# K chunks loaded in pairs wherever two neighbouring places come free within eight items

## The chip, the core and the metric

The kernel runs on one core of a Trainium2 chip. The core has engines with instruction streams of their own: PE (matmul, with its weight loads), DVE (vector), ACT (scalar), POOL, and SP (sync), which here only issues transfers. Sixteen DMA engines move the data between HBM and the on-chip memory. The metric is the device time of one execution in microseconds (us), lower is better.

## What is computed

Two layers, each an attention block over a cache followed by a small MLP block, for 8 sequences (batches) with one new token each, in bfloat16. Both layers read the same cache and the same weights.

```
q = (layernorm(x) @ wq)                    # 16 query heads of 256, 8 K/V heads, 2 query heads to each
scores = q . k_cache * 256**-0.5           # 4096 cached positions
o = softmax(scores) . v_cache
x = x + o @ wo                             # attention
h = gelu(layernorm(y) @ w1) ...            # MLP block B on y = layernorm(x); x = x + B(y)
x = attention; x = MLP; x = attention; x = MLP
```

With one position per sequence, the shifts in the MLP block bring in only zeros, so w1 and w2 add nothing and the kernel does not load them. The K and V caches are 8 x 8 x 4096 x 256 each, 128 MiB each.

## The kernel before

**Units, chunks and places.** The work is cut into units (layer `ps`, batch `b`, head pair `gp`): two K/V heads of one batch in one layer. A unit has four K chunks and four V chunks of 1 MiB (128 partitions by 8 KB). The on-chip memory holds `NC` = 17 places of one chunk each, side by side in one tile `places_t` (line 80), so two neighbouring places are one stretch of 16 KB per partition. A K chunk `c` holds, for each partition, the c-th 8 KB of a 32 KB run of the cache; so two neighbouring K chunks are 16 KB in a row in HBM too, and one transfer of 2 MiB can bring both, if two neighbouring places are free. Whole V chunks are 1 MiB transfers.

**What is kept.** Head pairs 2 and 3 (`keep`) of a batch are loaded in layer 0 and stay on the chip until layer 1 has used them: 14 of the 17 places hold them at the tightest point, a further V chunk is moved to PSUM (`inner`), and one is split between PSUM and the tile `rest` (`part`, `halfway`). Head pairs 0 and 1 (`free`) are loaded once for each layer.

**The list of items.** `block` and `first_kept` (lines 731 to 795) write out one list `items` of chunks in the order in which they are used. For each batch: units of `free` head pairs and the two kept units of layer 0; then a run of V chunks loaded as two halves of 512 KB (`narrow`, `halved`), under which the attention result of this batch goes through its output projection, the MLP and the next query (`chain`); then the kept K and V chunks again for layer 1, mixed with K chunks of the units that follow. I call the time from the kept chunks of layer 1 until the engines have caught up with the loads the catch-up.

**What an item does.** For a loaded K chunk, DVE transposes it in place (`transpose_k`, three instructions on line 1009). PE multiplies it with the query (`scores`, line 1024). For units named by `paired`, the scores wait for the second chunk of a pair and, where the two lie in neighbouring places, 32 matmuls of 256 columns do both; otherwise 64 of 128 columns. `late` says whose scores wait. Kept K chunks need no load and no transpose in layer 1; their first item's matmuls read both chunks of a pair. ACT takes the exponentials (line 1033). For a V chunk, PE multiplies the probabilities with it (line 1092).

**The list of loads.** `loads` is `items` without what is still on the chip. The main loop (line 1272) writes the instructions of one item, gives back the place or places that it used (lines 1463 to 1476), and calls `emit_loads` (line 930), which takes loads from the head of the list as long as it finds places. All of this is decided while the program is built: SP gets a fixed sequence of transfers, issued in order, each behind a wait for the last reader of its place. A transfer that waits holds up all behind it.

**How places are chosen.** For each place, `free_at` has the number of the item after which it comes free. `both_for` (line 900) looks whether a K chunk and its neighbour can be loaded as one: the mate must be among the next three loads, both places free or coming free within `AHEAD` = 4 items, and, where no pair is held yet, at least `QUEUED` = 7 loaded chunks still ahead of their use. The pair's places are then held, and `emit_loads` stops until both are free. Otherwise `place_for` (line 873) takes the first open place for the single chunk and may hold a neighbour for its mate, so that the scores can be done together although the chunks are loaded one by one. `paired` (line 850) excludes the units `begin[0]` and the last two of `final_units`.

At the start, `emit_loads(2)` issues the first two blocks of wq and `emit_loads(5)` (line 1133) five more transfers; then come the weights (lines 1134 to 1159), which are first used before item 12 (`kept_q`).

Of the kernel before, what the change touches and what calls it, by code (L numbers as in the profile page):

```python
# [17 lines left out]
def kernel(  # L18
# [27 lines left out]
    nc = tc.nc  # L46
# [3 lines left out]
    Dh = A_k_cache.shape[3]  # L50
# [10 lines left out]
    NC = 17  # L61
# [6 lines left out]
    PR = 6  # L68
# [10 lines left out]
    PB = 16 * Dh  # L79
    places_t = consts.tile([128, NC * PB], BF16, name="places")  # L80
    slots = [places_t[:, n * PB : (n + 1) * PB] for n in range(NC)]
    rest_t = consts.tile([128, (16 - PR) * Dh], BF16, name="rest")
# [603 lines left out]
    keep = sorted({gp for gp, _, _ in kept})  # L686
    free = [gp for gp in range(GP) if gp not in keep]
    assert Bn > 2 and free == [0, 1] and GP == 4
    begin = [(0, 0, 0), (0, 0, 1), (0, 1, 0), (0, 2, 0)]
# [10 lines left out]
    final_units = [(1, 5, 1), (1, 6, 1), (1, 7, 0), (1, 7, 1)]  # L700
# [18 lines left out]
    tasks, items, due = [], [], []  # L719
    number, narrow, halved, loose = {}, set(), set(), set()  # L720
# [101 lines left out]
    saved = {u for units in ahead for u in units}  # L822

    def stays(it):
        n, kv, c = it
        return (tasks[n][2], kv, c) in kept
# [5 lines left out]
    def halfway(it):  # L832
        n, kv, c = it
        return (tasks[n][2], kv, c) == part

    def here(it):

        return tasks[it[0]][0] == 1 and (stays(it) or inside(it) or halfway(it))

    loads = [it for it in items if not here(it)]  # L840


    places = list(range(NC))
    where = {}

    held = {}
    AHEAD = 4
    QUEUED = 7

    def paired(n, c):  # L850

        ps, _, gp = tasks[n]
        return gp in keep or tasks[n] in saved or tasks[n] in final_units[:2] + begin[1:]

    def late(it):

        n, kv, c = it
        return kv == 0 and paired(n, c) and not (tasks[n][0] == 1 and stays(it))
# [3 lines left out]
    used_at = {it: k for k, it in enumerate(items)}  # L862
# [7 lines left out]
    free_at = [-1] * NC  # L870
    now = [0]

    def place_for(it):

        n, kv, c = it
        if it in held:
            p = held.pop(it)
            if p not in places:
                held[it] = p
                return None  # L880
            places.remove(p)
        else:
            open_ = [p for p in places if p not in held.values()]
            if not open_:
                return None
            p = open_[0]
            if kv == 0 and c % 2 == 0 and paired(n, c):
                two = [
                    (max(free_at[q], now[0]), k, p1, q)
                    for k, p1 in enumerate(open_)  # L890
                    for q in (p1 + 1, p1 - 1)
                    if 0 <= q < NC and q not in held.values() and free_at[q] <= now[0] + AHEAD
                ]
                if two:
                    _, _, p, q = min(two)
                    held[n, 0, c + 1] = q
            places.remove(p)
        return p

    def both_for(it):  # L900

        n, kv, c = it
        mate = (n, 0, c + 1)
        if it not in held:
            if kv or c % 2 or not paired(n, c) or mate not in loads[:3]:
                return None
            open_ = [p for p in range(NC) if p in places or free_at[p] >= 0]
            two = [
                (max(free_at[q] if q not in places else -1 for q in (p, p + 1)), p)
                for p in open_  # L910
                if p + 1 in open_ and not {p, p + 1} & set(held.values())
            ]
            two = [t for t in two if t[0] <= now[0] + AHEAD]
            if not two or sum(used_at[i] > now[0] for i in where if i in used_at) < QUEUED:
                return None
            p = min(two)[1]
            held[it], held[mate] = p, p + 1
        if held.get(mate) != held[it] + 1:
            return None
        return held[it], mate  # L920

    def taken(it, p):

        where[it] = p
        n, kv, c = it
        if stays(it):
            where[tasks[n][1:], it[1:]] = p
        free_at[p] = again[tasks[n][1:], kv, c] if tasks[n][0] == 0 and stays(it) else used_at[it]

    def emit_loads(most=None):  # L930
        n = 0
        while loads and places and n != most:
            it = loads[0]
            both = both_for(it)
            if both:
                p, mate = both
                if p not in places or p + 1 not in places:
                    break
                for i, q in ((it, p), (mate, p + 1)):
                    loads.remove(i)  # L940
                    places.remove(q)
                    del held[i]
                    taken(i, q)
                _, b, gp = tasks[it[0]]
                nc.sync.dma_start(
                    places_t[:, p * PB : (p + 2) * PB],
                    A_k_cache[b, 2 * gp : 2 * gp + 2]
                    .rearrange("g s d -> (g s) d")
                    .rearrange("(p u z) d -> u p (z d)", u=2, z=32)[it[2] // 2],
                )  # L950
                n += 1
                continue
            p = place_for(it)
            if p is None:
                break
            del loads[0]
            taken(it, p)
            t, kv, c = it
            _, b, gp = tasks[t]
            dst = slots[p]  # L960
            n += 1
            if kv == 2:
                load_weights(dst, gp, b)
                continue
            rows = (A_v_cache if kv else A_k_cache)[b, 2 * gp : 2 * gp + 2].rearrange(
                "g s d -> (g s) d"
            )
            if kv:
                src = rows.rearrange("(a p y) d -> a p (y d)", a=4, y=16)[c]
            else:  # L970
                src = rows.rearrange("(p x y) d -> x p (y d)", x=4, y=16)[c]
            if halfway(it):
                nc.sync.dma_start(dst[:, 0 : PR * Dh], src[:, 0 : PR * Dh])
                nc.sync.dma_start(rest_t[:], src[:, PR * Dh :])
            elif loads and it not in halved:
                nc.sync.dma_start(dst, src)
            else:
                for y in range(2):
                    nc.sync.dma_start(
                        dst[:, 8 * Dh * y : 8 * Dh * (y + 1)], src[:, 8 * Dh * y : 8 * Dh * (y + 1)]  # L980
                    )

    def load_tail(dst, src):

# [4 lines left out]
    def load_weights(dst, kind, rows):  # L989

        if kind == "o":
            nc.sync.dma_start(
                dst[:, 0 : WI * D].rearrange("p (h x) -> p h x", x=2 * D),
                A_wo[0 : WI * 128].rearrange("(h p j) d -> p h (j d)", p=128, j=2),
            )
            return
        src = A_wq[:, HU * rows[0] : HU * rows[0] + HU]
        nc.sync.dma_start(
            dst[:, 0 : 3 * HU].rearrange("p (f c) -> p f c", f=3),
            src[0:384].rearrange("(f p) c -> p f c", f=3),  # L1000
        )
        load_tail(dst[:, 3 * HU : 3 * HU + HU // 2], src)
# [38 lines left out]
    def inner_words(slot):  # L1041

        return [(store[n][:], slot[:, 1024 * n : 1024 * n + 1024]) for n in range(4)]
# [228 lines left out]
    for idx, it in enumerate(items):  # L1272
# [9 lines left out]
        n, kv, c = it  # L1282
        ps, b, gp = tasks[n]
# [9 lines left out]
        kept_now = here(it)  # L1293
        p = where[(b, gp), (kv, c)] if kept_now else where[it]
# [3 lines left out]
        if kv == 2:  # L1298
            rows = b
# [25 lines left out]
        elif kv == 0:  # L1325
# [23 lines left out]
            x = c - c % 2  # L1349
# [4 lines left out]
            elif scored:  # L1354
                two = [
                    where[(b, gp), (0, k)] if kept_now else where[n, 0, k] for k in (x, x + 1)
                ]
# [14 lines left out]
        else:  # L1372
# [15 lines left out]
            if final and gp in free:  # L1388
                pv_cols(oc, slot, c, gp, psv[slot_of[n]])
                if c % 2 == 1:  # L1390

                    u = c // 2
# [70 lines left out]
        if kv == 2:  # L1463
            if gp == "q" or rows is not None:
                places.append(p)
        elif not (ps == 0 and stays(it)):
            if (ps, gp, kv, c) == (1, keep[1], 1, homes[0]):
                where[(b, part[0]), part[1:]] = p
                moves.extend(part_words(slot))
            elif (ps, gp, kv, c) == (1, keep[1], 1, homes[1]):  # L1470
                where[(b, inner[0]), inner[1:]] = p
                moves.extend(inner_words(slot))
            elif not late(it):
                places.append(p)
            elif c % 2:
                places.extend([where[n, 0, c - 1], p])
# [24 lines left out]
    for q in range(4):  # L1501
        for fc in range(4):
            at = min(128 * fc, D - 128)
# [134 lines left out]
```

## Time and profile before

| what | value |
|---|---|
| runs | 1037.08, 1040.58, 1041.28 us; median 1040.58 |
| profiled execution | 1038.57 us, its span 1036.0 us |
| moved by SP's queue | 419.66 MB in 73296 packets |
| HBM read over the span | 405 GB/s |
| mean granted clock of PE | 0.614 |
| K transfers of 2048 KB / 1024 KB | 49 / 94 |
| V transfers of 1024 / 512 KB | 87 / 194 |

The profile is one execution; its span runs from the first to the last instruction of the program. Engine shares are busy times over the span. "DMA" in the row of slices is the mean busy share of the sixteen DMA engines, "GB/s" what they moved in each of 40 slices of 25.9 us. In a row of instructions, "x" is the count, then busy us and the mean ns of one; behind the bar stands the idle time before them and what ended it. SP's waits for places are not a loss by themselves: as long as earlier transfers are queued, the DMA engines have work.

### The profile page before, as it was taken

The numbers are of one execution on the slowest core, as the hardware profiler recorded it, in microseconds if no ns is written. First come the engines' busy times: TensorE is split into PE (matmuls) and PEld (weight loads), VectorE is DVE, ScalarE is ACT, GpSimd is POOL, SyncE is SP. The second block draws the span as 40 slices with busy tenths as digits, with TensorE's granted clock in tenths as the row PEclk, the third lists the DMA queues.
The fourth block names the chain that finished last, engine by engine and source line by source line (L and its number), as shares of the span: only waits on it lengthen the run. The fifth ranks groups of instructions, "written<-read, shape, count | busy, mean of one in ns | idle before, by whom it ended". The sixth has DMA issues, their size and how long they took to land. (4 is left out here: it accounts for less than half of the span.)

```text
span 1036.0 us, 29893 instructions
## 1 busy us (share of the span) xinstructions
PE 668.8 (65%) x13219; PEld 429.1 (41%) x13219; DVE 597.9 (58%) x1407; ACT 211.5 (20%) x685; POOL 16.3 (2%) x27
## 2 busy tenths in 40 slices
PE   3154545875677557766775677567756774677775
PEld 2022322553345334533453345335533552345555
DVE  7054577258725971597259725782597259725582
ACT  1011111141214120412041214121412141214110
POOL 0000000000000000000000000000000000000000
PEclk9975555565667566655665565566555665556555
DMA  9999999999999999999999999999999999999994
GB/s 361 396 425 422 423 422 419 393 421 419 419 401 421 422 417 382 419 422 419 401 415 425 417 402 411 421 417 388 418 420 418 401 419 423 417 402 408 413 419 198
DMA packets 73472, 421.56 MB, mean 407 GB/s; under 512 B 7544, under 2 KB 13440, under 8 KB 43904
## 3 DMA queue, kind: packets, MB, share of 16 engines
q1 hardware_dynamic: 73296, 419.66, 99.1%
q8 instruction: 103, 1.69, 0.7%
q14 instruction: 25, 0.20, 0.0%
q10 hardware_dynamic: 48, 0.01, 0.0%
HBM read 419.63 MB, written 0.01 MB: 405 GB/s over the span
## 5 line engine op out<-in xcount | busy, mean ns | idle before, releaser
L1009 DVE STREAM_TRANSPOSE places<-places 128x512 uint32<-128x512 uint32 (+1 forms) x576 | 455.5, 854 | 58.8 <-DMA places<-in_A_k_cache_dram 58.6
L1024 PE MATMUL sc<-places,qbd 128*8 128x256 bf16 (+1 forms) x5248 | 248.8, 342 | 175.4 <-DVE places L1009 168.5
L1092 PE MATMUL o<-places,ptw 128*8 128x256 bf16 x3808 | 243.7, 380 | 111.5 <-DMA places<-in_A_v_cache_dram 82.2
L1024 PEld LDWEIGHTS <-qbd 128*8 128x8 bf16 x5248 | 134.0, 105 | 247.0 <-DVE places L1009 130.6
L1092 PEld LDWEIGHTS <-ptw 128*8 128x8 bf16 x3968 | 103.9, 102 | 175.1 <-issue 99.0
L1033 ACT ACTIVATE p_n<-sc 128x256 bf16<-128x256 f32 x128 | 95.5, 746 | 341.2 <-PE sc L1024 335.7
L1267 ACT COPY ptw<-psv 128x32 bf16<-128x32 bf16 x248 | 53.1, 227 | 175.0 <-PE o L1092 173.0
L415 DVE CAST qbd<-misc 32x16 bf16<-32x16 f32 (+1 forms) x184 | 30.8, 167 | 63.2 <-PE misc L409 61.4
L592 PE MATMUL misc<-R_t,o_t 128*128 128x4 f32 (+1 forms) x212 | 45.5, 321 | 29.2 <-DVE qbd L415 12.8
L592 PEld LDWEIGHTS misc<-R_t,o_t 128*128 128x128 f32 x212 | 41.2, 271 | 45.2 <-issue 17.3
L1082 ACT CAST psv<-misc 128x128 bf16<-128x128 f32 x64 | 17.0, 265 | 198.8 <-PE misc L1075 198.8
L532 DVE RECIPROCAL rz<-misc 128x4 f32<-128x4 f32 (+1 forms) x55 | 9.7, 176 | 80.4 <-PE misc L529 43.6
L1060 ACT COPY places<-store 128x1024 bf16<-128x1024 bf16 x40 | 40.2, 1029 | 11.2 <-PE o L1092 10.7
L529 PE MATMUL misc<-zm,one 128*128 128x4 f32 (+1 forms) x110 | 28.0, 326 | 15.0 <-DVE zm L521 12.6
L529 PEld LDWEIGHTS misc<-zm,one 128*128 128x128 f32 x110 | 23.2, 263 | 30.8 <-DVE zm L521 15.9
L180 PEld LDWEIGHTS <-w_sb 128*128 128x128 bf16 x896 | 27.5, 104 | 15.7 <-issue 15.7
L1033 ACT ACTIVATION_READ_ACCUMULATOR p_n<-sc 128x1 f32 x128 | 33.8, 264 | 0.0
L546 ACT COPY o_t<-o 128x256 f32<-128x256 f32 x53 | 19.7, 373 | 49.5 <-PE o L1092 49.5
L295 POOL TENSOR_TENSOR t<-t,nhalf 128x2 f32<-128x2 f32 (+2 forms) x18 | 12.0, 669 | 955.5 <-DVE t L316 955.5
L1075 PEld LDWEIGHTS <-p_n 128*128 128x128 bf16 x256 | 11.9, 105 | 32.4 <-issue 20.9
L1055 DVE TENSOR_SCALAR store<-places 128x512 uint32<-128x512 uint32 x40 | 25.0, 679 | 0.0
L1075 PE MATMUL misc<-identb,p_n 128*128 128x32 bf16 x256 | 18.1, 191 | 10.3 <-ACT p_n L1033 6.8
(158 smaller groups left out, 358.7 us busy)
## 6 DMA issues: line engine op xcount, KB each, us to landing
places<-in_A_k_cache_dram SPq DMA_DIRECT2D x49, 2048.0 KB, 17.2
places<-in_A_v_cache_dram SPq DMA_DIRECT2D x194, 512.0 KB, 7.2
places<-in_A_k_cache_dram SPq DMA_DIRECT2D x94, 1024.0 KB, 12.0
places<-in_A_v_cache_dram SPq DMA_DIRECT2D x87, 1024.0 KB, 20.9
places<-in_A_wq_dram SPq DMA_DIRECT2D x7, 768.0 KB, 9.8
rest<-in_A_v_cache_dram SPq DMA_DIRECT2D x8, 640.0 KB, 18.5
places<-in_A_v_cache_dram SPq DMA_DIRECT2D x8, 384.0 KB, 14.8
wo_sb<-in_A_wo_dram SPq DMA_DIRECT2D x1, 2688.0 KB
```

The costliest lines, as they stand in the source:

```text
L180: nc.tensor.matmul(bass.AP(out.tensor, out.offset, [out.ap[0], (1, WIDE)]), w, x.to_broadcast([128, WIDE]), start=start, stop=stop, skip_g ...
L415: nc.vector.tensor_copy(qbd[32 * a : 32 * a + 32, :, g0 : g0 + ng, a, :], qs.rearrange("p e (f g u h) -> p (e f) u g h", f=2, u=2, h=2)[:, ...
L529: nc.tensor.matmul(z_ps, ones, zm[:], start=True, stop=True)
L592: nc.tensor.matmul(ot_ps[:, j], o_sb[:].rearrange("p (i j) -> p j i", j=2)[:, j], R, start=True, stop=True)
L1009: nc.vector.transpose(w, w)
L1024: nc.tensor.matmul(sc[32 * k : 32 * k + 8, 128 * (x % 2) : 128 * (x % 2 + nx)], qbd[:, ep, gp % 2].rearrange("p a h -> p (a h)"), v, start ...
L1033: nc.scalar.activation(p_sb[:, :, :, 2 * u : 2 * u + 2].rearrange("p t i x -> p x t i"), sc[:, 0:256].rearrange("p (x t i) -> p x t i", x= ...
L1055: nc.vector.tensor_single_scalar(kept_words.bitcast(U32), words.bitcast(U32), 0, op=ALU.bitwise_or)
L1060: nc.scalar.copy(words, kept_words.bitcast(BF16))
L1075: nc.tensor.matmul(pt_ps[:, t], p_sb[:, t].rearrange("p i x -> p (i x)"), cols, start=True, stop=True,)
L1092: nc.tensor.matmul(o_ps[32 * q : 32 * q + 8, :], ptz[:, at : at + 8], v[:, y * Dh : (y + 1) * Dh] if v2 is None or y < PR else v2[:, (y - ...
L1267: nc.scalar.copy(ptw[:, ring_of[it], :, 6:8], psv[slot_of[it[0]]][:, it[2]])
```

## The change

The two functions `place_for` and `both_for` go; `open_places`, `pick` and `reserve` come, and the issue of a K or V load moves to functions of its own.

- A pair may be held if both places are free or come free within `SOON` = 8 items (4 before); a held pair whose places are not free yet needs `QUEUED` = 5 chunks ahead (7 before); the mate must be among the next four loads.
- `paired` now has all of `final_units` and `begin`.
- A single chunk takes the open place with the fewest open neighbours, so that neighbours stay together. It no longer holds a place for its mate.
- A K chunk 1 that is loaded alone takes chunk 2 with it, if that is next or next but one in the list and the place behind it is open.
- Of a kept pair in layer 1, both places are given back after the first of its two items.
- `emit_loads(5)` counts transfers as before, and a pair is one of them.

By the order of both programs, K transfers of 2048 KB are 86 (49 before) and of 1024 KB 20 (94 before); V transfers and weights are the same in number and size. SP's first five transfers after the two wq blocks were five K chunks; now they are three K pairs, one V chunk and one K pair. After each batch's halved V chunks stood mostly singles (eight in the first two batches); now one single, one pair, one single, and pairs with V chunks between. PE has 960 score matmuls of 128 columns fewer (2304 to 1344) and 480 of 256 more (2944 to 3424).

```diff
-    AHEAD = 4
-    QUEUED = 7
+    SOON = 8
+    QUEUED = 5
...
-        return gp in keep or tasks[n] in saved or tasks[n] in final_units[:2] + begin[1:]
+        return gp in keep or tasks[n] in saved or tasks[n] in final_units + begin
...
+    def pick(open_):
+        return min(open_, key=lambda p: ((p - 1 in open_) + (p + 1 in open_), p))
+
+    def reserve(it, mate):
+        open_ = open_places()
+        taken_ = set(held.values())
+        def at(p):
+            return max(-1 if q in places else free_at[q] for q in (p, p + 1))
+        two = [
+            p
+            for p in range(NC - 1)
+            if not {p, p + 1} & taken_
+            and all(q in places or 0 <= free_at[q] <= now[0] + SOON for q in (p, p + 1))
+        ]
+        if not two:
+            return
+        p = min(two, key=lambda p: (at(p), sum(q in open_ for q in (p - 1, p + 2)) % 2, p))
+        queued = sum(used_at[i] > now[0] for i in where if i in used_at)
+        if at(p) <= now[0] or queued >= QUEUED:
+            held[it], held[mate] = p, p + 1
...
     def emit_loads(most=None):
         n = 0
         while loads and places and n != most:
             it = loads[0]
+            k, kv, c = it
+            mate = (k, 0, c + 1)
+            if kv == 0 and c % 2 == 0 and paired(k, c) and mate in loads[:4]:
+                if it not in held:
+                    reserve(it, mate)
+                if it in held:
+                    p = held[it]
+                    if p in places and p + 1 in places:
+                        del held[it], held[mate]
+                        taken(it, p)
+                        taken(mate, p + 1)
+                        load_k(it, p, 2)
+                        n += 1
+                        continue
+                    break
+            open_ = open_places()
+            if not open_:
+                break
+            p = pick(open_)
+            taken(it, p)
...
+                both = c == 1 and (k, 0, 2) in loads[:2] and p + 1 in open_
+                if both:
+                    taken((k, 0, 2), p + 1)
+                load_k(it, p, 1 + both)
...
+            elif kv == 0 and kept_now:
+                if c % 2 == 0:
+                    places.extend([p, where[(b, gp), (0, c + 1)]])
             elif not late(it):
                 places.append(p)
```

More of the change, by code (lines that the diff above doesn't have):

```diff
@@ L871 @@
     now = [0]
[L873 to L916, printed above, removed]
+    def open_places():
+        return [p for p in places if p not in held.values()]
@@ L917, in both_for @@
             held[it], held[mate] = p, p + 1
-        if held.get(mate) != held[it] + 1:
-            return None
-        return held[it], mate
     def taken(it, p):
@@ L928, in taken, with load_k, load_v @@
         free_at[p] = again[tasks[n][1:], kv, c] if tasks[n][0] == 0 and stays(it) else used_at[it]
+        if kv == 2 and tasks[n][1] is None:
+            free_at[p] = -1
+        loads.remove(it)
+        places.remove(p)
+    def load_k(it, p, n):
+        _, b, gp = tasks[it[0]]
+        rows = A_k_cache[b, 2 * gp : 2 * gp + 2].rearrange("g s d -> (g s) d")
+        nc.sync.dma_start(
+            places_t[:, p * PB : (p + n) * PB],
+            rows.rearrange("(p z) d -> p (z d)", z=64)[:, it[2] * PB : (it[2] + n) * PB],
+        )
+    def load_v(it, dst):
+        _, b, gp = tasks[it[0]]
+        rows = A_v_cache[b, 2 * gp : 2 * gp + 2].rearrange("g s d -> (g s) d")
+        src = rows.rearrange("(a p y) d -> a p (y d)", a=4, y=16)[it[2]]
+        if halfway(it):
+            nc.sync.dma_start(dst[:, 0 : PR * Dh], src[:, 0 : PR * Dh])
+            nc.sync.dma_start(rest_t[:], src[:, PR * Dh :])
+        elif loads and it not in halved:
+            nc.sync.dma_start(dst, src)
+        else:
+            for y in range(2):
+                nc.sync.dma_start(
+                    dst[:, 8 * Dh * y : 8 * Dh * (y + 1)], src[:, 8 * Dh * y : 8 * Dh * (y + 1)]
+                )
     def emit_loads(most=None):
@@ L933, in emit_loads @@
             it = loads[0]
[L934 to L937, printed above, removed]
-                    break
[L939 to L952, printed above, removed]
@@ L953, in emit_loads @@
-            p = place_for(it)
-            if p is None:
+            k, kv, c = it
[12 more added lines that the diff above has]
+                        continue
+                    break
@@ L955, in emit_loads @@
+            open_ = open_places()
+            if not open_:
                 break
-            del loads[0]
+            p = pick(open_)
             taken(it, p)
-            t, kv, c = it
-            _, b, gp = tasks[t]
-            dst = slots[p]
             n += 1
             if kv == 2:
[L963 to L967, printed above, removed]
@@ L968, in emit_loads @@
-            if kv:
-                src = rows.rearrange("(a p y) d -> a p (y d)", a=4, y=16)[c]
-            else:
[L971 to L981, printed above, removed]
+                load_weights(slots[p], tasks[k][2], tasks[k][1])
+            elif kv:
+                load_v(it, slots[p])
+            else:
+                both = c == 1 and (k, 0, 2) in loads[:2] and p + 1 in open_
+                if both:
+                    taken((k, 0, 2), p + 1)
+                load_k(it, p, 1 + both)
```

## The prediction

> **What bounds the kernel now.** I read the page first, its busy shares and its row of transfer rates; then the chain that ended last; then the busy times of two long stretches; then the sync engine's own timeline at the place where its queue is shortest.
>
> ```profile
> PE 668.8 (65%) x13219; PEld 429.1 (41%) x13219; DVE 597.9 (58%) x1407; ACT 211.5 (20%) x685; POOL 16.3 (2%) x27
> ...
> DMA  9999999999999999999999999999999999999994
> GB/s 361 396 425 422 423 422 419 393 421 419 419 401 421 422 417 382 419 422 419 401 415 425 417 402 411 421 417 388 418 420 418 401 419 423 417 402 408 413 419 198
> ...
> q1 hardware_dynamic: 73296, 419.66, 99.1%
> ...
> places<-in_A_k_cache_dram SPq DMA_DIRECT2D x49, 2048.0 KB, 17.2
> ...
> places<-in_A_k_cache_dram SPq DMA_DIRECT2D x94, 1024.0 KB, 12.0
> ```
>
> No engine is busy for more than 65% of the span, while the transfers of SP's one queue (q1) fill 99.1% of what the sixteen DMA engines have, and every slice but the last shows a 9. What differs from slice to slice is the rate: 415 to 425 GB/s for most, 382 to 402 where each batch's V chunks are loaded in halves of 512 KB. The chain of waits agrees:
>
> ```profile
> 967.31 19.25 DMA places<-in_A_v_cache_dram
> 986.64 21.09 DMA places<-in_A_v_cache_dram
> 1007.79 17.29 DMA places<-in_A_v_cache_dram
> 1025.09 0.05 issue
> ```
>
> The last V chunk is in at 1025.09, and 1036.0 - 1025.1 = 10.9 us of short steps on PE, DVE and ACT follow. So the time is the length of one stream of 419.66 MB plus that tail. The bytes don't change. The change can win in two ways only, by a better rate or by fewer pauses, and lose by more pauses.
>
> **Term 1: larger transfers.** By the order of the programs, 49 K transfers of 2048 KB become 86 and 94 of 1024 KB become 20: 37 pairs take the place of 74 singles. V transfers (87 whole, 194 halves, 8 in two parts) and weights are the same in number and size. What a pair saves I take from two stretches: 972 to 1012 us moves 1 MiB chunks (with one weight block of 0.9 MB); 42 to 122 us repeats one 2 MiB pair and two 1 MiB V chunks, half of the bytes in pairs.
>
> ```profile
> core 0: us, PE busy (x) PEld busy (x) DVE busy (x) ACT busy (x) POOL busy (x), PEclk, DMA share, GB/s
> 972.00:1012.00 40.00, 29.65 (x716) 22.17 (x717) 27.07 (x67) 5.95 (x23) 1.99 (x2) 0.57 1.01 419
> 42.00:122.00 80.00, 38.04 (x614) 21.36 (x615) 40.07 (x77) 11.10 (x42) 0.00 (x0) 0.65 1.01 424
> ```
>
> The last column is the rate. 1.049 MB at 419 GB/s is 2.503 us, two are 5.005. For the mixed stretch 1/424 = 0.5/r + 0.5/419, so r = 429 GB/s, and a pair of 2.097 MB takes 4.887 us: 0.118 us less. Times 37 that is **-4.4 us**. The rates are rounded; with 423.5 against 419.5 it is -3.5, with 424.5 against 418.5 it is -5.2. I keep these as ends.
>
> [...]
>
> **Term 2: pauses of the stream.** A held pair stops the list (the loop breaks), and since SP issues in order, every load behind it, K, V and weights alike, waits for both places. That costs nothing while earlier transfers are queued. I laid the list of issues of the changed program beside the old one, item by item, and at each issue took the bytes that it has queued less than the old one. Most often the queue ends up the same or 2 MiB (4.9 us) shorter, where the old one was 5 to 20 us long (from issue to first packet in the trace). It is nearly used up at one place, in the fifth batch:
>
> ```profile
> 634.79 0.33 SPq L945 DMA_DIRECT2D places<-in_A_k_cache_dram  x1
> 635.17 1.86 SPq L976 DMA_DIRECT2D places<-in_A_k_cache_dram  x2
> 642.96 0.33 SPq L976 DMA_DIRECT2D places<-in_A_v_cache_dram  x1
> 647.53 0.33 SPq L945 DMA_DIRECT2D places<-in_A_k_cache_dram  x1
> ```
>
> The old program issues a pair, two singles and a V chunk here before the next pair. The new one issues the first pair and then nothing until the V chunk whose place its next pair needs has been used; on PE those products are
>
> ```profile
> 644.93 0.85 PE L1092 MATMUL o<-rest,ptw 128*8 128x256 bf16 x10
> ```
>
> and end at 645.8. The first pair landed 13.4 us after its issue (the 2048 KB row of the DMA issues in this stretch), at 648.2 on its slowest DMA engine; by the packets the middle engine was done with it at about 645.5. So the queue meets the new issue with -0.3 to +2.4 us to spare. What an issue needs until its first packet is no row by itself; the shortest in the trace is 0.6 us, for the issue at 621.6. I charge **+1 us** here, between 0 (slowest engine) and 2 (middle engine and 1 to 2 us of start). At the other six batches the same count leaves 0.8 to 2.5 us at the worst issue, more than that 0.6; I charge nothing, and up to 0.5 us each, +3, as the high end.
>
> **Edits that I cost at nothing.** Both places of a kept pair given back at once: the first item's 32 matmuls already read both chunks, so the second place comes free at the same matmul; what changes is that one 2 MiB issue may stand there instead of two (the load after the half chunks was the shortest queue of before, 0.6 to 2.1 us in each batch, and its first single is still there). *Matmuls:* 15 more score pairs lie side by side, 960 of 128 columns become 480 of 256. By the two forms' rows (78.6 us for 2304, 170.1 us for 2944) PE does 32.8 - 27.7 = 5 us less, and 480 weight loads of 25.5 ns (134.0 over 5248) go, 12 us; both lie under the stream, and DVE, not PE, paces the catch-up after each batch (35.8 of the 40 us from 222 to 262). Transposes stay at 576. Should the cover go, these are gains. *Start:* the first five issues hold 9 MB of cache instead of 5, so the weights behind them come some 4.2 MB, 10 us, later. The V chunk before which they are first used lies behind them in both orders, with the same bytes ahead of it; the K chunks come earlier. *End:* the last K chunk is followed by nine V chunks instead of eight, and the last transfer is the same halved V, so the 10.9 us tail stays. *Fewer issues:* 37 times 0.33 us of SP, which waits anyway.
>
> **Sum:** -4.4 + 1 = -3.4 us. The profiled execution took 1038.57 us, of which 2.6 lie around the span of 1036.0; from it 1035.2. It lies 2.0 us under the median of the runs shown, 1040.58, from which it would be 1037.2. I give the middle, **1036.2 us**.
>
> **Rivals.**
> *Size doesn't matter:* the two stretches differ for another reason (a weight block, how busy PE and DVE are), and 1 MiB chunks run as fast as pairs. For it: a stretch where K singles come one after another, 212 to 226 us, shows 422 GB/s. Against: the mixed one holds 424 over 80 us. Then only the pause is left: 1038.57 + 1 = 1039.6, 1040.6 on the middle base. [...]
> *More is won:* the high end of term 1, -5.2, no pause, and the slow half-chunk stretches of two batches (382 and 388 GB/s against 401 in the others, 25.9 us wide: 1.2 + 0.8 us) come back to the others' rate because their queue is fuller when they begin. That is -7.2: 1032.4. Against: the half chunks themselves are loaded as before.
> *The queue runs dry, and it is slower:* the place is the catch-up after each batch's kept chunks, where the old program fills single places as they come free and the new one waits for neighbours. Price: a second place comes free one K item after the first, three transposes at 854 ns, 2.6 us; if two of some five new pairs in each of seven batches find the queue empty and wait 1 us beyond it, 14 us are lost: 1038.57 - 4.4 + 14 = 1048.2. It decides over term 1 from 4.4 us of pauses in all, and over the bound of slower from 9.6, or 1.4 us a batch. For it: queues of 0.8 to 2.5 us by my count at the worst issue of each batch. Against: each is still above zero but one.
> That the change doesn't do what it says is excluded: the order shows 86 pairs.
>
> **How the numbers follow.** 0.5% of the median is 5.2 us, about what a measurement of this kernel can tell from no change. Forecast 0.52, size doesn't matter 0.07, more is won 0.25, queue dry 0.16. The forecast's own spread (the runs shown lie 4 us apart) puts 0.10 of its 0.52 beyond 5.2 us. So faster 0.25 + 0.10 = 0.35, same 0.42 + 0.07 = 0.49, slower 0.16. The range reaches from 1031 (more is won, less 1.4) to 1043 (forecast from the median with +3 of further pauses, and half the runs' spread); it leaves out most of the dry queue and little else.
>
> **What would show it.** The issues row: 86 K transfers of 2048 KB, 20 of 1024. The slices outside the half chunks at 420 to 426 GB/s instead of 415 to 425, and the same 382 to 402 inside. The last V chunk in at about 1021.7 and the tail still 10.9 us. About the fifth batch, near 643 us, one slice with a DMA share visibly below the rest for about 1 us. I would be wrong if a slice after a batch's half chunks falls below 410 GB/s in each batch (dry queue), or if the rate stays at 419 where pairs are loaded (size).

## The result and the profile after

The changed kernel takes **1036.83 us** (median of 13 runs, 1035.19 to 1037.61); the kernel before, run beside it, 1039.47 us (13 runs, 1037.08 to 1041.49). The ratio is 0.9976, its 95% interval 0.9967 to 0.9985: 2.64 us less, real but inside the 0.5% that I called "the same". The forecast was 1036.2 us.

The profiled execution of the changed kernel took 1035.63 us, 2.94 less than that of before. From its page come the busy times, the DMA engines' share and rate in 40 slices, the totals of the transfers, and the issues by kind:

```profile
span 1033.6 us, 28857 instructions
...
PE 655.7 (63%) x12739; PEld 417.7 (40%) x12739; DVE 597.4 (58%) x1407; ACT 211.6 (20%) x685; POOL 16.4 (2%) x27
...
DMA  9999999999999999999999999999999999999994
GB/s 364 390 426 420 423 423 419 390 424 424 416 402 422 424 417 401 419 425 398 407 412 425 418 399 412 423 418 399 426 424 416 401 414 425 418 401 411 418 422 199
DMA packets 68141, 421.51 MB, mean 408 GB/s; under 512 B 6952, under 2 KB 12848, under 8 KB 43312
...
q1 hardware_dynamic: 67968, 419.66, 99.1%
...
places<-in_A_k_cache_dram SPq DMA_DIRECT2D x86, 2048.0 KB, 14.3
...
places<-in_A_k_cache_dram SPq DMA_DIRECT2D x20, 1024.0 KB, 11.8
```

The same 419.66 MB go through the same queue, which is as full as before (99.1%); it needs 67968 packets instead of 73296, mostly since 37 pairs more bring 16 KB in a packet where two packets brought 8 KB each. Read the rates slice by slice against the row of before. Of the 32 slices outside the half chunks, 20 have gained 1 to 8 GB/s, five are equal and seven have lost. The eight with half chunks (each fourth one from the eighth on) lie at 390 to 407; two that were the lowest have risen, 382 to 401 and 388 to 399 (whether the change does that is taken up with the limit of 4 chunks below). One slice has clearly lost: the nineteenth, 465 to 491 us, 398 where 419 stood. PE is busy for 13 us less and its weight loads for 11 us less.

The chain that ended last (start, length, what) has kept its end:

```profile
979.69 25.08 DMA places<-in_A_v_cache_dram
1004.78 17.69 DMA places<-in_A_v_cache_dram
1022.48 0.05 issue
```

The last V chunk is in 2.61 us earlier than before (1025.09), and 1033.6 - 1022.5 = 11.1 us follow, against 10.9. So the whole gain lies in the stream of transfers.

### The profile page after: what moved, and what is told of

It is laid out like the page before. It is cut to its first block, busy times and chain, and to the rows that moved or that the text cites. A ratio compares the mean times of both kernels' runs of the same rounds, so it can differ in the third digit from the quotient of the medians.

```text
span 1033.6 us, 28857 instructions
## 1 busy us (share of the span) xinstructions
PE 655.7 (63%) x12739; PEld 417.7 (40%) x12739; DVE 597.4 (58%) x1407; ACT 211.6 (20%) x685; POOL 16.4 (2%) x27
## 3 DMA queue, kind: packets, MB, share of 16 engines
q1 hardware_dynamic: 67968, 419.66, 99.1%
## 4 chain that ended last, share of the span: by engine, by line
DMA 43%; DVE 27%; PE 22%; issue 3%; SPq 3%; ACT 2%; POOL 0%; DVEq 0%; ACTq 0%
DMA places<-in_A_v_cache_dram 28%; DVE places L1000 22%; DMA places<-in_A_k_cache_dram 14%; PE sc L1015 9%; PE o L1083 6%; PE misc L592 2%; PE misc L180 2%; ACT p_n L1024 2%; DVE qbd L415 1%; DVE store L1046 1%; DMA places<-in_A_wq_dram 1%; PE misc L529 1%; SPq L932 1%; SPq L199 1%; PE misc L1066 1%
## 5 line engine op out<-in xcount | busy, mean ns | idle before, releaser
L1015 PE MATMUL sc<-places,qbd 128*8 128x256 bf16 (+1 forms) x4768 | 236.3, 352 | 164.8 <-DVE places L1000 163.9
L1015 PEld LDWEIGHTS <-qbd 128*8 128x8 bf16 x4768 | 124.2, 105 | 231.6 <-DVE places L1000 123.5
L592 PE MATMUL misc<-R_t,o_t 128*128 128x4 f32 (+1 forms) x212 | 45.5, 321 | 29.1 <-DVE qbd L415 12.4
L596 DVE CAST qT<-misc 128x8 bf16<-128x8 f32 (+1 forms) x37 | 7.2, 195 | 27.0 <-PE misc L592 20.3
```

The source lines that it names most:

```text
L592: nc.tensor.matmul(ot_ps[:, j], o_sb[:].rearrange("p (i j) -> p j i", j=2)[:, j], R, start=True, stop=True)
L1015: nc.tensor.matmul(sc[32 * k : 32 * k + 8, 128 * (x % 2) : 128 * (x % 2 + nx)], qbd[:, ep, gp % 2].rearrange("p a h -> p (a h)"), v, start ...
```

## The experiments

Two things were open: whether the gain comes from the size of the transfers or from something else that the change moves (order, places, matmuls), and whether the held pairs cost pauses. In all that follows a difference is that of a kernel's median from the kernel before, run on the same chip at the same time.

**Each pair as two transfers, in the changed kernel and in the one before.**

```diff
-        nc.sync.dma_start(places_t[:, p * PB : (p + n) * PB], ...)
+        for k in range(n):
+            nc.sync.dma_start(places_t[:, (p + k) * PB : (p + k + 1) * PB], ...)
```

> The changed kernel, its places, order and moments of issue kept, but each of the 86 K pairs goes out as two transfers of 1 MiB one behind the other (8 KB runs). If the gain comes from larger transfers (term 1, 0.118 us a pair): 86 x 0.118 = 10.1 us more than the changed kernel, 1036.8 + 10.1 = 1046.9 us, ratio to before 1.007. If size does not matter, and the gain came from where the places are, from fewer score matmuls or from places given back at once: 1036.8 us again, ratio 0.997.

Measured: 1042.87 us, ratio 1.003 (1.0017 to 1.0043), 3.14 us over before. Against the changed kernel, 2.64 under before, that is 5.8 us for 86 pairs, 0.067 us a pair: the size of transfers counts, at little more than half of my 0.118. The same edit of the kernel before, with its 49 pairs:

> The kernel before, its 49 pairs as two singles each: 192 K transfers of 1 MiB, as in the changed kernel with two singles (1042.9 us), but in the order and places of before. If a pair is worth 0.07 us (6.0 us over 86 pairs): 1039.6 + 3.4 = 1043.0 us. If it is worth the 0.118 us of the prediction: 1045.4 us. If order, places and fewer score matmuls do something by themselves, it ends away from 1042.9 us: above it if they help.

Measured: 1042.29 us, ratio 1.0027 (1.0016 to 1.0037), 2.63 over before, 0.054 a pair. With all pairs split the two kernels lie 0.5 us apart (+3.14 and +2.63), which these intervals cannot tell from nothing. So what else the change does, order, places, matmuls, kept places given back at once, makes no difference that shows.

**The change with the old limits.** The new code holds as few pairs as the old if it is given the old numbers:

```diff
-    SOON = 8
-    QUEUED = 5
+    SOON = 4
+    QUEUED = 7
```

> The changed kernel with the two limits of before (places free within 4 items, 7 chunks queued): by the program's order 49 K pairs and 94 singles, the numbers of before, with the new choice of places, the new list of paired units and the kept places given back at once. If the number of pairs makes the gain: as before, ratio 1.000 within 0.002. If the other parts of the change make it: 0.9976 as the changed kernel.

Measured: 1040.06 us, ratio 1.001 (0.9998 to 1.0021). The 49 pairs and 94 singles of before come back, and with them its time. Both ways of asking give one answer: the number of pairs makes the gain.

**One transfer, but short runs.** A pair differs from two singles in two respects: one transfer instead of two, and 16 KB in a row per partition instead of 8. To part them, the pair stays one transfer of 2 MiB, with its two chunks named in reverse order, so that no 16 KB are in a row:

```diff
+        if n == 2:
+            dst = bass.AP(dst.tensor, dst.offset + PB, [dst.ap[0], (-PB, 2), (1, PB)])
+            src = bass.AP(src.tensor, src.offset + PB, [src.ap[0], (-PB, 2), (1, PB)])
```

> The changed kernel, each of the 86 pairs still one transfer of 2 MiB, but written as two runs of 8 KB per partition (the second chunk first), so that the run is as short as a single's. It parts the length of a run from the size of a transfer, which the two halves by partition did not. If the run's length is what pays: near the two singles, 1042.9 us, less at most 0.8 us for 86 completions fewer, and the packets of pairs are of 8 KB at some 314 ns. If the size of the transfer pays: 1036.8 us as the changed kernel.

Measured: 1042.16 us, ratio 1.0025 (1.0014 to 1.0036), 2.50 over before, as two singles (+3.14) and not as the changed kernel (-2.64). Its page has the 86 transfers of 2048 KB and the packets of two singles:

```profile
DMA packets 79149, 421.51 MB, mean 405 GB/s; under 512 B 6952, under 2 KB 12848, under 8 KB 43312
...
places<-in_A_k_cache_dram SPq DMA_DIRECT2D x86, 2048.0 KB, 14.5
```

The reversed order costs nothing that shows: by the packet records an 8 KB packet takes 315.5 ns on the mean here and 315.6 in the changed kernel with two singles. So it is the length of the run, the packet of 16 KB, and not the size of the transfer or the number of issues.

**The other way to part them failed.** A pair as two transfers with long runs, 64 partitions each:

```diff
+        for k in range(n):
+            half = slice(128 // n * k, 128 // n * (k + 1))
+            nc.sync.dma_start(places_t[half, p * PB : (p + n) * PB], ...)
```

> The changed kernel, but each K pair goes out as two transfers of 64 partitions, each 1 MiB with runs of 16 KB. It parts the length of a run from the size of a transfer. If long runs are what makes pairs cheap: as the changed kernel, 1036.8 us, at most 0.5 us more for 86 more transfers. If the size of a transfer does it: as the two singles, about 1046.9 us. If size does not matter at all: 1036.8 us, and the two singles too.

Measured: 1603.33 us, the median of six runs from 1581.16 to 1624.95; the ratio of 1.527 (1.5217 to 1.5328) is that of the three shortest. No theory had this. Its page:

```profile
DMA packets 69517, 421.52 MB, mean 262 GB/s; under 512 B 8328, under 2 KB 14224, under 8 KB 44688
...
q1 hardware_dynamic: 69344, 419.66, 98.0%
```

The queue is nearly as full as before, 98.0% against 99.1%, but the kernel moves 262 GB/s where before moves 407: here busy engines are not fast ones. By the packet records a 16 KB packet takes 1210 ns on the mean here, 617 in the kernel before. So these transfers over 64 neighbouring partitions ran at about half the rate, and this kernel says nothing on sizes.

**The price by itself.** This kernel has transfers only: chunks of the caches into places in turn, nothing waits for any computation, all computation is left out and zeros are written. Five stretches: K singles, K pairs, half chunks, V pairs, V singles.

```diff
+    stream(A_k_cache, range(0, 16), 1)
+    stream(A_k_cache, range(16, 32), 2)
+    halves(A_k_cache, range(0, 16))
+    stream(A_v_cache, range(0, 16), 2)
+    stream(A_v_cache, range(16, 32), 1)
```

> The disputed cost by itself: nothing but transfers, 64 MiB of cache in each of five stretches, into sixteen places in turn: K as 1 MiB singles (8 KB runs), K as 2 MiB pairs (16 KB runs), K as halves of 512 KB (4 KB runs), V as pairs, V as singles. It leaves out all computation and writes zeros. With term 1 as predicted (0.118 us a pair) pairs run at 429 GB/s against 419; with 0.07 us, as the two singles gave, at 425 against 419. The halves: 400 GB/s if it is the 4 KB run that slows the stretches of halved V chunks, over 410 if it is their short queue.

Measured: 802.43 us, one run. The busy times of the five stretches, in that order; the last column is the rate:

```profile
core 0: us, DVE busy (x) POOL busy (x), PEclk, DMA share, GB/s
4.00:156.00 152.00, 0.00 (x0) 0.00 (x0) 1.00 1.01 423
166.00:310.00 144.00, 0.00 (x0) 0.00 (x0) 1.00 1.01 428
320.00:480.00 160.00, 0.00 (x0) 0.00 (x0) 1.00 1.03 410
485.00:630.00 145.00, 0.00 (x0) 0.00 (x0) 1.00 1.01 428
645.00:790.00 145.00, 0.00 (x0) 0.00 (x0) 1.00 1.01 422
```

Pairs run at 428 GB/s, singles at 422 to 423, half chunks, with runs of 4 KB, at 410. In the two V stretches the packet records give 421.9 and 428.4, so a pair of 2.097 MB saves 4.970 - 4.895 = **0.075 us**, and 37 of them 2.8 us. The pairs' rate is what I had inferred (429); the singles' was not the 419 of my first stretch (why, is said below). The halves settle neither theory: of the way from 422 down to the kernel's 390 to 407, their 410 shows 12 GB/s without any short queue. Their runs are shorter and their transfers smaller at once, so which of the two it is, stays open.

**The kept places one by one.**

```diff
-            elif kv == 0 and kept_now:
-                if c % 2 == 0:
-                    places.extend([p, where[(b, gp), (0, c + 1)]])
```

> The changed kernel, but the two places of a kept pair are given back one by one, as before: by the order 78 pairs and 36 singles. If the number of pairs makes the gain: 8 pairs fewer at 0.118 us, 1036.8 + 0.9 = 1037.7 us, ratio 0.998. If giving back both at once is what fills the queue after the half chunks: back to before, ratio 1.000, and the queue at the first load after the half chunks shorter than in the changed kernel.

Measured: 1038.4 us, ratio 0.9989 (0.9978 to 0.9999), 1.33 under before, with 78 pairs and 36 singles. It lies between before and the changed kernel. Eight pairs at 0.075 are 0.6 us of the 1.3 by which it falls short; the rest is within the intervals.

**What waiting can cost.** Three kernels move the limit of queued chunks, and one that of items. First, a pair is always waited for:

```diff
-    QUEUED = 5
+    QUEUED = 0
```

> The changed kernel with a pair held however few chunks are queued (limit 0 instead of 5): by the program's order 95 pairs and 2 singles. If pairs pay and the queue does not matter: 9 x 0.07 = 0.6 us less than the changed kernel, 1036.2 us. If waiting for a pair with a short queue stops the stream (the rival of the prediction that ends slower): the first loads after the half chunks, with 1 to 2 us queued, wait; at least 1.5 us in each of seven batches, 1036.8 + 10.5 = 1047 us or more, and the DMA share falls below 1 there.

Measured: 1043.37 us, ratio 1.0032 (1.002 to 1.0044): with 95 pairs, the most of all, 3.71 over before. The slice from 543 to 569 us is down at 337 GB/s, and the stretch where it is lost says why:

```profile
core 0: us, PE busy (x) PEld busy (x) DVE busy (x) ACT busy (x) POOL busy (x), PEclk, DMA share, GB/s
544.00:552.00 8.00, 3.26 (x60) 1.85 (x59) 7.68 (x15) 1.06 (x4) 0.00 (x0) 0.57 0.43 177
```

For more than half of these 8 us the DMA engines have nothing to do. In the changed kernel the same stretch has a share of 1.01 and 424 GB/s. The wait was expected in each of seven batches; besides this one, two shorter pauses stand after the half chunks of two others (shares of 0.72 from 732 to 736 us and 0.79 from 832 to 836).

Second, the old limit of 7 chunks with the new one of 8 items:

> The changed kernel with its old limit of 7 queued chunks and the new one of 8 items: by the order 78 pairs and 36 singles. If only the number of pairs counts: 8 pairs fewer at 0.07 us, 1036.8 + 0.6 = 1037.4 us. If the short queue of the changed kernel costs as much as its last pairs bring (its slice from 465 us moves 398 GB/s where before moved 419, 1.3 us): 1036 us, and that slice back at 415 or more.

Measured: 1042.19 us, ratio 1.0024 (1.001 to 1.0039), 2.20 over before, with 78 pairs. Both theories had 1036 to 1037.4, and both miss. The loss is at the same place: the stretch, SP's own timeline there (start, length, line, what, count), and SP's waits from 530 to 556 us (what for, us in total, times, longest):

```profile
544.00:552.00 8.00, 3.69 (x88) 2.51 (x88) 7.97 (x12) 1.05 (x4) 0.00 (x0) 0.50 0.55 194
```

```profile
529.54 20.06 SPq L918 DMA_DIRECT2D places<-in_A_k_cache_dram  x4
549.64 0.71 SPq L932 DMA_DIRECT2D places<-in_A_v_cache_dram  x1
```

```profile
SPq L918 <- DVE places L1000: 16.2, 3, 10.4
```

SP stands for up to 10.4 us at a K load whose place DVE has not yet done with; behind it stands a V load, issued only at 549.64. DVE is busy for 7.97 of the 8 us, transposing what has landed. By then the queue is used up. In the changed kernel two of the singles ahead of this are one pair, and other places come free for what follows: the last K pair ahead of the V load goes out at 541.33 (here at 549.26), and the V load at 541.70:

```profile
526.27 15.38 SPq L918 DMA_DIRECT2D places<-in_A_k_cache_dram  x5
541.70 0.43 SPq L932 DMA_DIRECT2D places<-in_A_v_cache_dram  x1
550.58 0.33 SPq L918 DMA_DIRECT2D places<-in_A_k_cache_dram  x1
```

Here too SP stands still, from 542.1 to 550.6, but with that V chunk and the loads ahead of it already queued, and the stretch shows no loss. So a stricter limit is not a safer one: a pair that is not held changes which places are open later, and the wait turns up elsewhere.

Third, a limit of 4 chunks, which changes one place in the last batch:

> The changed kernel with 4 queued chunks asked for instead of 5: its order differs at one place alone, in the last batch, where two singles become a pair (87 pairs). A control for the one before: no difference that can be measured from the changed kernel (0.1 us less by pairs), 1036.8 us, unless that one pair makes the queue run dry near 940 us, which would show as a slice below 400 GB/s there.

Measured: 1036.86 us, ratio 0.9988 (0.9977 to 0.9998), with 87 pairs. The changed kernel has 1036.83 us and 0.9976; the intervals overlap, and the last batch shows no dip. Up to that place, near 930 us, the two programs are the same, order and places too, so their profiles show what changes from one execution to the next:

```profile
GB/s 369 389 424 422 422 425 418 399 417 424 416 381 424 424 414 373 421 424 405 407 416 426 418 402 405 423 418 398 424 422 417 397 418 424 418 399 410 416 422 198
```

The twelfth and the sixteenth slice, both of half chunks, have 381 and 373 GB/s here and 402 and 401 in the changed kernel's profile. So a dip among half chunks comes and goes with the execution, and the rise of two such slices from before to after is not shown to be the change's. The nineteenth slice is low in both (405 and 398, where before had 419).

And pairs within 12 items:

```diff
-    SOON = 8
+    SOON = 12
```

> The changed kernel with places that come free within 12 items instead of 8: its order differs at two places alone, in the fourth and in the seventh batch, where two singles become a fourth pair in a row (88 pairs, 16 singles). If pairs pay wherever they are: 2 x 0.09 = 0.2 us less than the changed kernel, 1036.6 us. If it is the wait for neighbours that stopped the stream at 544 to 552 us in the kernel that always waits: the same pause of some 4 to 5 us stands here in the slice from 543 us, and 1036.8 + 4.5 = 1041.3 us or more.

Measured: 1040.65 us, ratio 1.0022 (1.0012 to 1.0032), 2.37 over before, with 88 pairs. Slower, as the theory of waits had it, but not where it said: from 544 to 552 us the DMA share is 0.97. Its profiled execution, at 1044.38 us the longest of its runs, dips at two other places:

```profile
704.00:708.00 4.00, 4.00 (x66) 2.52 (x67) 0.51 (x3) 0.60 (x4) 0.00 (x0) 0.50 0.88 305
708.00:712.00 4.00, 3.02 (x55) 1.84 (x52) 1.77 (x10) 0.26 (x2) 0.70 (x1) 0.50 0.85 258
```

```profile
770.00:774.00 4.00, 3.06 (x53) 1.28 (x45) 3.52 (x7) 1.12 (x5) 0.00 (x0) 0.50 0.63 203
```

In the second stretch the engines idle for a third of 4 us, and a K pair and a V load behind it are issued only at 772.09 and 772.47: the pattern of the two kernels above. The list of transfers in this batch is that of the changed kernel, which issues the same pair at 757.91. But that the order differs "at two places alone" holds for the list only: by the programs, the chunks take other places from the fourth batch on, and loads go out at other items. The dips from 704 to 712 lie among half chunks, whose loads wait for PE's products (14.7 us of SP's waits from 700 to 732), with PE granted 0.50 throughout. Such a dip needs no change of the kernel: the run with 4 queued chunks has one at 392 to 396 us (286 GB/s, a share of 0.89, PE granted 0.50), where the changed kernel, by the same program, has 383 and 1.04 in its profile. That the granted clock brings these dips is not shown.

**Whole V chunks in place of halves**, to see what the half chunks hold back:

```diff
-        halved.update(due[: n + 2])
```

> The changed kernel, but the V chunks after the layer-0 units, 96 of them, come as one transfer of 1 MiB (8 KB runs) instead of two of 512 KB (4 KB runs). If the run's length pays at 4 KB too: 400 against 419 GB/s is 2.62 against 2.50 us a chunk, 0.118 x 96 = 11.4 us, 1036.8 - 11.4 = 1025.4 us. If the queue is too short for it (PE begins a chunk 1.3 us later, the place comes free later, and the queue there is some 3.3 us): pauses take it back, 1036 us or more.

Measured: 1052.34 us, ratio 1.0132 (1.0107 to 1.0156), 12.68 over before. The runs are longer, 8 KB for 4, and the rate of those slices goes down:

```profile
GB/s 374 388 426 425 421 423 414 343 421 424 418 338 417 425 417 377 414 418 402 364 420 407 408 363 407 422 420 361 397 422 422 371 409 422 421 387 408 416 421 191
```

Where the changed kernel has 390 to 407, this one has 338 to 387. So the half transfers, short runs and all, are worth keeping there. That it is the short queue that costs, as I had expected, is argued: from 290 to 317 us the DMA share is 0.95 at 342 GB/s, so idle time is less than half of the loss; by the packet records an 8 KB packet takes 364 ns there on the mean, where it takes 314 in the kernel before from 42 to 122 us.

## Why the prediction came out as it did

**What bounds the kernel: right.** The queue is 99.1% full in both; the gain is a better rate of the same bytes, and the last V chunk's landing carries all of it. I named 1021.7 us for it and a tail of 10.9; they are 1022.5 and 11.1.

**Term 1, larger transfers: right in kind, too large.** This is the term that was mis-sized. Predicted were 0.118 us a pair and -4.4 us for 37, with ends of -3.5 and -5.2. Measured by itself, a pair saves 0.075 us, so -2.8; inside the kernels 0.067 (86 pairs) and 0.054 (49), so -2.5 and -2.0. All lie outside my ends. The error was the rate taken for singles, 419 GB/s. I had put a weight block of 0.9 MB into that stretch; by the packet records there is none, all 2035 data packets of its loads have 8 KB. What is in it besides is the queue that brings the program's instructions, here from 972 to 1012 and from 42 to 122 us (packets, MB, share of the engines):

```profile
q8 instruction: 6, 0.10, 1.0%
```

```profile
q8 instruction: 5, 0.08, 0.4%
```

The loads' own 416.8 GB/s in 99.0% of the time are 421, those of the mixed stretch 424.7, and from these two a pair saves 0.087 us, -3.2 in all. What is left above 0.075 is less than 1 GB/s: with the mixed stretch as it is, each GB/s in the singles' rate is worth some 0.024 us a pair, 0.9 us of the term. The row that I gave the rival, K singles one after another at 422, was the better one: with it the same mixed stretch gives 426 for pairs and a term of -1.7, and with the 428 measured since, -2.6. I had it in hand and used it only as an argument. My ends came from the rounding of two rates, which was not the larger doubt.

**Term 2, pauses: right in size, wrong in place.** I charged 1 us in the fifth batch near 643 us. The 1 to 2 us of start in its upper end were an estimate: in the trace of before the K load issued at 621.61 us has its first packet at 622.57 (0.6 us after its instruction's end, the count of the prediction), and SP's first transfer, issued at 0.74, has it at 1.85, so 1.0 and 1.1 us are shown, and 2 us by no run. In the fifth batch a stretch of 10 us shows this, before and then after:

```profile
641.00:651.00 10.00, 8.32 (x167) 5.21 (x160) 6.25 (x14) 4.94 (x12) 0.00 (x0) 0.50 1.00 419
```

```profile
641.00:651.00 10.00, 7.40 (x203) 5.47 (x193) 7.00 (x15) 4.55 (x11) 0.00 (x0) 0.67 0.99 408
```

(419 - 408) / 419 times 10 is 0.26 us, and the run with 4 queued chunks, by the same program, has 422 there, so not even this is sure. What is lost lies in the fourth batch, at a place that I had charged nothing; before, after, and the run with 4 queued chunks:

```profile
463.00:482.00 19.00, 12.02 (x236) 6.80 (x235) 17.78 (x25) 3.62 (x11) 0.00 (x0) 0.59 1.01 422
```

```profile
463.00:482.00 19.00, 11.10 (x200) 6.07 (x192) 17.85 (x26) 3.94 (x12) 0.00 (x0) 0.59 0.99 393
```

```profile
463.00:482.00 19.00, 10.68 (x192) 5.99 (x195) 17.25 (x25) 2.91 (x9) 0.00 (x0) 0.59 1.00 404
```

(422 - 393) / 422 times 19 is 1.3 us, and 0.8 with 404; of the 1.3 the stretches beside it (437 to 463 and 482 to 491 us, 4 to 5 GB/s faster than before) give 0.35 back. It is hardly a pause: by the packet records the engines idle for 0.2 us only, and a 16 KB packet takes 653 ns on the mean where it took 616. SP waits for DVE here as in the kernels with true pauses, 10.7 us in two waits, but that the short queue makes the packets slow is only argued. The two slices of half chunks that rose, by 1.2 and 0.7 us, do not belong in the sum, since such dips change with the execution. So the sum after the fact is -2.8 for the pairs and +1.0 for the fourth batch, -1.8, where the medians lie 2.64 apart (1.6 to 3.4 by the interval of the ratio); the 0.8 between the two is within what the runs cannot tell. That the forecast of 1036.2 us came so near to 1036.83 is in part luck: the pairs bring 1.6 us less than I had put in, and the runs came out 0.8 us better than the terms that I can show.

**Edits at nothing: right together.** With the pairs split (+3.14 against +2.63) and with the old limits (1.001) the rest of the change comes out within 0.5 us of nothing. That PE is busy for 13 us less, where I had counted 5 (12.4 of it in the score matmuls, whose mean times fell as well, from 389 to 383 ns and from 282 to 274, at a mean granted clock of 0.631 for 0.614), and its weight loads for 11, where I had counted 12, lies under the stream, as said.

**The rivals.** *Size doesn't matter* falls: singles cost 0.054 to 0.075 us a pair more in each of the three ways it was measured. A transfer of 2 MiB with runs of 8 KB is no faster than two of 1 MiB as far as the intervals tell (ratios of 1.0025 and 1.003 to before), and one with runs of 16 KB is, by 1.2 to 1.5% of its time (0.060 us of 4.97 between the changed kernel and the one with the reversed order, 0.075 alone). *More is won* is not borne out: the two lowest slices of the half chunks did rise to the others' rate in the profile, by the 2 us that it gave them, but the run with 4 queued chunks has such low slices again; and the rival's 5.2 us for the pairs were twice what they bring. *The queue runs dry* did not decide this kernel but is real: three neighbouring settings (limits of 0 and of 7 chunks, and 12 items) end 2.2 to 3.7 us over before, with pauses in their traces, in one to three batches and not in each. That the changed limits stay clear of it my count of the queue at each issue had told, but for the fourth batch; that 7 in place of 5 does not, I did not foresee.

## What to carry to other kernels

When one stream of transfers fills the span, count the bytes that lie in a row per partition and not only the bytes per transfer (shown here for 8 and 16 KB, at 1 and 2 MiB over 128 partitions: 422 to 423 and 428 GB/s). Take the rate of each kind from a stretch that holds this kind alone, and see which queues are in it. Before a rise of one slice is put down to a change, hold it against a second profile of the same program. Waiting for a longer run pays about 0.07 us a pair here, and a pause like the one at 544 us (0.45 of 8 us idle, 3.6 us) takes back fifty pairs: before loosening or tightening such a limit, go through the list of issues for what stands behind the wait. None of the settings tried beats the changed kernel.

## What the hardware showed that I had not expected

In the kernel with pairs cut by partitions, a transfer over 64 neighbouring partitions ran at about half the rate, with all sixteen DMA engines shown as busy (98.0% of the span, 262 GB/s on the mean, 1210 ns for a packet of 16 KB instead of 617), though the other half was queued right behind it. What makes these packets slow, no run shows. And the rate went by the length of the run: 422 to 423 GB/s with 8 KB and 428 with 16 KB, in a kernel of transfers alone (410 with 4 KB, there in transfers of 512 KB).
